# Two early stores cut into 112, 8 and 8 rows, and the last third of q and k in three loads instead of two

## The chip, the cores and the metric

One core of a Trainium2 chip runs the whole program. The metric is device time in microseconds (us), median of several executions. The kernel before takes 254.43 us (three executions: 254.37, 254.43 and 254.54).

The engines are named as in the profile: PE is TensorE (matmuls), PEld its weight loads, DVE is VectorE, ACT is ScalarE, POOL is GpSimd and SP is SyncE. Sixteen DMA engines move the data between memory and SBUF.

## What is computed

Four batches of cross-covariance attention, and a mixture of low-rank adapters on their result:

```python
B, N, C = 4, 6400, 256                      # q, k, v: float32 [B, N, C]
qn = q / (norm(q, axis=1) + 1e-06)          # over the 6400 rows
kn = k / (norm(k, axis=1) + 1e-06)
s = kn.transpose(0, 2, 1) @ qn / tau        # [B, 256, 256]
a = softmax(s, axis=-1)
x = (v @ a).reshape(B * N, C)               # [25600, 256]

logits = x @ w_gate                         # 8 experts
# the two best experts of each row, softmax over the two as weights w
out = x + sum over those two of  w * (x @ A[e]) @ B[e]      # A[e]: 256x16, B[e]: 16x256
```

The norms and the product of a batch need all of its q and k; only then is `a` known, and each row of v can be finished. So for each batch the kernel loads q and k (13.1 MB together in float32), accumulates the Gram products, makes `a`, and then streams v through to the output.

## The kernel before

A list scheduler written in Python at the top of the kernel makes a plan of steps (loads, matmuls, copies, stores), each with an engine and an estimated duration, and simulates them. The order in which its simulation starts the steps is the order in which they are emitted; on each engine the instructions then stand in that fixed order. Changing one load changes the simulation and with it the order of the steps from there on.

The 6400 rows of a batch are laid out as 128 partitions of 50 columns, a column being 256 elements of one row. q and k come in thirds of 17, 17 and 16 columns, v and the output in five pieces of 10 columns:

```python
NC = 50
PC = 10
QK = ((0, 17), (17, 17), (34, 16))
V = ((0, 1), (1, 1), (2, 1), (3, 1), (4, 1))
...
STORE = {"zl": 1, "bank": 6, "qk": 6, "v": 3, "vT": 4, "y": 7, ...}   # buffers of each kind
```

Some thirds are cut further. `PARTS` says how, by batch and third; everything else comes in one load. FINE cuts the last two output pieces:

```python
PARTS = {(0, 0): ((0, 2), (2, 15)), (0, 2): ((34, 8), (42, 8)), (3, 2): ((34, 8), (42, 8))}
FINE = 2
```

In the plan, each part is one load for q and one for k, and the Gram step of a column depends on the part that holds it:

```python
        for c, n in PARTS.get((b, i), QK[i:i + 1]):
            for h in "qk":
                p.add(("load", h, b, i, c, n), {}, (), 0, take=(("qk", (h, b, i)),), size=LOAD * n + 0.062)
...
            for c in range(c0, c0 + n):
                deps = [k for k in p.steps if k[0] == "load" and k[2:4] == (b, i) and k[1] != "v"
                        and k[4] <= c < k[4] + k[5]]
                ...
                p.add(("G", b, c), {"PE": ...}, deps, ...)
```

Loads of q, k and v are issued by GpSimd and cast float32 to bf16 on the way:

```python
    def do_load(s, what, b, i, c, n):
        ...
        nc.gpsimd.dma_start(t[:, c - c0:c - c0 + n, :], src[b, :, c:c + n, :])
```

Some output stores are held back until a given load of k has landed: `HOLD` names the store and the load. A held store stands in SyncE's order behind a tiny DMA that reads the last column of that load, so SyncE waits for it:

```python
HOLD = {(0, 0): ('k', 3, 1), (0, 1): ('k', 1, 2), (0, 4): ('k', 3, 2), (1, 0): ('k', 3, 1),
        (1, 1): ('k', 3, 2), (1, 2): ('k', 3, 2), (1, 3): ('k', 3, 2), (1, 4): ('k', 3, 2),
        (2, 0): ('k', 3, 1), (2, 1): ('k', 3, 2), (2, 4): ('k', 3, 1)}
...
    def do_hold(s, kind, b, i):
        if kind == "k":
            src = held["qk", ("k", b, i), ""][0:1, QK[i][1] - 1, 0:16]
        ...
        nc.sync.dma_start(scrap, src)
```

The store itself is one DMA of 128 partitions (rows, in what follows) from SyncE; a row of a whole piece is 10 columns of 256 float32, 10,240 bytes that lie together in memory:

```python
    out_v = out.rearrange("(b p c) d -> b p c d", b=B, p=P)
...
    def do_store(s, b, i, c, n):
        lo = i * PC + c
        nc.sync.dma_start(out_v[b, :, lo:lo + n, :], held["y", (b, i), ""][:, c:c + n, :])
```

The steps that follow the loads of a batch's q and k, as the profile names them: Gram products (`acc<-qk`), squares on ScalarE (`sq`, `ssq`), their sums on VectorE, the exponentials (`a_exp`), the gate and adapter weights times `a` (`waA`), transposes of v (`T_ps`), the gate's logits (`log`, `ZL`), the gate on VectorE (`gatem` to `gateg`), the low-rank part (`Z`, `gz`, `gzT`), the output product (`Y_ps`) and its copy to SBUF (`y`).

Of the kernel before, what the change touches and what calls it, by code (L numbers as in the profile page):

```python
# [32 lines left out]
class Clock:  # L33


    WINDOW, FIRST, LOW, HIGH = 3.413, 0.31, 0.5, 0.8

# [3 lines left out]
    def at(self, t):  # L41
        w = max(0, int((t - self.FIRST) / self.WINDOW) + 1)
        while len(self.cold) <= w:
            share = self.busy[-1] / self.WINDOW
            self.cold.append(share < (self.HIGH if self.cold[-1] else self.LOW))
            self.busy.append(0.0)
        return w

    def took(self, t, us):

        end, w = t, self.at(t)
        while us > 1e-9:
            pace = 2.0 if self.cold[w] else 1.0
            step = min(us * pace, max(self.FIRST + w * self.WINDOW - end, 1e-6))
            self.busy[w] += step
# [5 lines left out]
    def idle(self, t):  # L61

        w = self.at(t)
        return t - self.FIRST - (w - 1) * self.WINDOW - self.busy[w] > self.SPARE

# [165 lines left out]
def make_plan(B, order, ahead):  # L231
# [6 lines left out]
    for kind, b, i in order:  # L238
        if kind == "v":
            p.add(("load", "v", b, i, V[i][0] * PC, V[i][1] * PC), {}, (), 0, take=(("v", (b, i)),),  # L240
                  size=LOAD * V[i][1] * PC + 0.062)
            continue
# [5 lines that stand above are left out]
        p.add(("cast", h), {"ACT": 0.6}, [("load", h, 0, 0) + PARTS[0, 0][0]], 0)  # L248
    p.loads[2].size += 0.5
    for b in range(B):  # L250

        for i, (c0, n) in enumerate(QK):
# [3 lines that stand above are left out]
                if (b, c) < (0, PARTS[0, 0][0][1]):  # L256
                    deps = [("cast", k[1]) for k in deps]
# [32 lines left out]
        if b == 0:  # L290
            p.add(("wts",), {"DVE": 1.8}, [("load", "k", 0, len(QK) - 1) + PARTS[0, len(QK) - 1][1]], -200)

# [89 lines left out]
    for b in range(B):  # L382
        for i in range(NP):
            x = pos["v", b, max(g for g, (i0, _) in enumerate(V) if i0 <= i)]
            parts = UNITS if b == B - 1 and i >= NP - FINE else ((0, PC),)
            for c, n in parts:
# [23 lines left out]
        (1, 1): ('k', 3, 2), (1, 2): ('k', 3, 2), (1, 3): ('k', 3, 2), (1, 4): ('k', 3, 2),  # L410
        (2, 0): ('k', 3, 1), (2, 1): ('k', 3, 2), (2, 4): ('k', 3, 1)}

PARTS = {(0, 0): ((0, 2), (2, 15)), (0, 2): ((34, 8), (42, 8)), (3, 2): ((34, 8), (42, 8))}
FINE = 2
FIRST = 4
OFF = {(0, 0, 'k'), (0, 0, 'q'), (0, 1, 'q'), (0, 2, 'k'), (0, 2, 'q'), (0, 4, 'q'), (0, 5, 'q'),
        (0, 6, 'k'), (0, 6, 'q'), (0, 7, 'k'), (0, 8, 'q'), (1, 0, 'k'), (1, 0, 'q'), (1, 1, 'q'),
# [41 lines left out]
def kernel(  # L459
# [11 lines left out]
    nc = tc.nc  # L471

    B, N, C = q.shape
    P = 128
# [15 lines left out]
    out_v = out.rearrange("(b p c) d -> b p c d", b=B, p=P)  # L490
# [44 lines left out]
    held = {}  # L535
# [25 lines left out]
    def do_load(s, what, b, i, c, n):  # L561
        if what == "v":
            t, src, c0 = sb(s, "v", (b, i), [P, PC * max(n for _, n in V), C], BF16), v_v, c
        else:
            t = sb(s, "qk", (what, b, i), [P, max(n for _, n in QK), C], BF16)
            src, c0 = {"q": q_v, "k": k_v}[what], QK[i][0]
            if (b, c) == (0, 0):
                n = FIRST
                if "first" not in W:
# [6 lines left out]
        if (what, b, i) in (("q", 0, 0), ("k", 0, 0)):  # L576
            c, n = FIRST, c + n - FIRST
        nc.gpsimd.dma_start(t[:, c - c0:c - c0 + n, :], src[b, :, c:c + n, :])  # L578
# [346 lines left out]

    def do_store(s, b, i, c, n):
        lo = i * PC + c
        nc.sync.dma_start(out_v[b, :, lo:lo + n, :], held["y", (b, i), ""][:, c:c + n, :])


    do = dict(load=do_load, wts=do_wts, sq=do_sq, add=do_add, red=do_red, n2p=do_n2p, hold=do_hold, warm=do_warm, cast=do_cast, G=do_G, accs=do_accs, n2=do_n2, rsqrt=do_rsqrt, rq_ps=do_rq_ps, s=do_s,
              exp=do_exp, recip=do_recip, aT_ps=do_aT_ps, aT=do_aT, waA_ps=do_waA_ps, waA=do_waA,
              a=do_a, ZL=do_ZL, ZLe=do_ZLe, T=do_T, Te=do_Te, log=do_log, loge=do_loge, Z=do_Z, Ze=do_Ze, gzT=do_gzT,
              gzTe=do_gzTe, Y=do_Y, Ye=do_Ye, store=do_store)
    for name in ("m1", "eq1", "lm", "m2", "mask", "msum", "t", "th", "g2"):
        do[name] = gate_step(name)
# [50 lines left out]
```

## Time and profile before

The profile is of one execution with a span of 252.7 us from the first to the last instruction of the program.

| | |
|---|---|
| time, median of 3 | 254.43 us |
| PE busy | 217.8 us (86%) |
| DVE busy | 192.7 us (76%) |
| ACT busy | 151.1 us (60%) |
| POOL busy | 27.1 us (11%) |
| HBM read / written | 78.91 MB / 26.21 MB |
| mean granted TensorE clock | 0.986 |
| the last load of k, columns 42 to 49 of the last batch | landed at 182.94 us |
| the last matmul | ended at 246.8 us |
| the last store | issued at 247.42, landed at 251.95 us |

How to read it. The busy time of an engine is an average over stages, and a high one does not make the engine the bound. The slices of the page cut the span into 40 equal parts; a digit is the busy share in tenths. The DMA row is the mean share of the sixteen DMA engines, and the GB/s row counts the bytes of their packets. Section 3 splits the DMA time by queue: q0 carries what GpSimd issues (the loads), q1 what SyncE issues (nearly all stores), q10 what ScalarE issues, and q8 is the fetching of instructions. A DMA has landed when all its engines have reported; the trace holds the time of each of the sixteen reports, so one can see how far the engines of one DMA lie apart. SyncE does no computing: its waits are listed apart, and they tell what its stores, and at the end the program, waited for.

### The profile page before, as it was taken

The page shows a single profiled execution, that of the slowest core. Times are in us where ns is not written, and L with a number is a line of the kernel's source. Part 1 is how long each engine was busy: PE and PEld are TensorE (multiplying, and loading weights), DVE is VectorE, ACT ScalarE, POOL GpSimd, SP SyncE. Part 2 cuts the span into 40 slices and gives each one's busy share as a digit, 9 for nine tenths or more (in the row PEclk, how much of TensorE's full clock was granted, in tenths as well). Part 3 has the DMA queues.
Part 4 walks back from the last instruction along what each step waited for, and adds up shares of the span by engine and source line. Part 5 has one row for each costly group of instructions (what it writes and reads, how often), then busy time and mean ns, then how long its engine had stood idle before and what let it go on. Part 6 is the DMA issues. An engine that isn't in the chain of part 4 may idle for free.

```text
span 252.7 us, 5852 instructions
## 1 busy us (share of the span) xinstructions
PE 217.8 (86%) x2357; PEld 193.0 (76%) x2357; DVE 192.7 (76%) x528; ACT 151.1 (60%) x269; POOL 27.1 (11%) x54
## 2 busy tenths in 40 slices
PE   0274995988999998689999999889999979999990
PEld 0162882876999996579899899779999769999980
DVE  0055589869899987588899899489898898889850
ACT  5454427546786543975667768362674846657671
POOL 7003010040002002000500100500000000000000
PEclk9998899999999999999999999999999999999997
DMA  8999999999999999999999999999999999999996
GB/s 251 217 217 209 211 223 208 217 218 215 215 217 241 303 305 298 224 213 221 210 215 220 215 217 217 211 212 313 317 251 353 322 341 317 337 392 415 404 408 249
DMA packets 11243, 66.70 MB, mean 264 GB/s; under 512 B 1360, under 2 KB 1744, under 8 KB 6608
## 3 DMA queue, kind: packets, MB, share of 16 engines
q0 software_dynamic: 6912, 38.80, 74.4%
q1 hardware_dynamic: 3968, 26.87, 26.1%
q10 hardware_dynamic: 336, 0.66, 0.8%
q8 instruction: 18, 0.29, 0.4%
q14 instruction: 9, 0.07, 0.1%
HBM read 78.91 MB, written 26.21 MB: 416 GB/s over the span
## 4 chain that ended last, share of the span: by engine, by line
PE 53%; DMA 32%; issue 5%; DVE 4%; ACT 2%; POOL 1%; POOLq 0%; DVEq 0%
DMA v<-in_v_dram 18%; PE Y_ps L915 13%; PE acc L593 10%; DMA qk<-in_q_dram 10%; PE Y_ps L920 6%; PE T_ps L788 5%; PE ZL_ps L812 5%; DMA qk<-in_k_dram 5%; PE gzT_ps L902 4%; PE acc L597 3%; PE acc L602 2%; PE Z_ps L879 1%; ACT a_exp L715 1%; DVE a_bf L763 1%; PE log_ps L826 1%
## 5 line engine op out<-in xcount | busy, mean ns | idle before, releaser
L593 PE MATMUL acc<-qk 128*128 128x256 bf16 x400 | 69.6, 282 | 17.0 <-DMA qk<-in_k_dram 9.4
L915 PE MATMUL Y_ps<-a_bf,vT 128*128 128x256 bf16 x400 | 60.0, 273 | 0.2 <-DVE acc_sb L710 0.2
L621 DVE TENSOR_TENSOR ssq<-ssq,sq 128x1280 f32<-128x1280 f32 (+1 forms) x27 | 43.4, 1606 | 19.6 <-ACT sq L615 19.6
L769 ACT COPY y<-Y_ps 128x512 f32<-128x512 f32 x79 | 46.2, 586 | 16.6 <-PE Y_ps L920 13.5
L593 PEld LDWEIGHTS <-qk 128*128 128x128 bf16 x400 | 34.2, 101 | 20.7 <-DMA qk<-in_k_dram 11.5
L615 ACT ACTIVATE sq<-qk 128x1280 f32<-128x1280 bf16 (+1 forms) x27 | 36.9, 1368 | 17.7 <-DVE ssq L621 16.6
L915 PEld LDWEIGHTS <-vT 128*128 128x128 bf16 x400 | 38.9, 98 | 4.7 <-issue 0.3
L920 PE MATMUL Y_ps<-ball,gzT 128*128 128x256 bf16 x200 | 38.2, 273 | 0.0
L597 PE MATMUL acc<-qk 128*128 128x128 bf16 x242 | 34.5, 224 | 0.0
L788 PE MATMUL T_ps<-ident,v 128*128 128x128 f32 x200 | 27.6, 274 | 0.6 <-DVE waA_sb L757 0.4
L769 ACT COPY vT<-T_ps 128x512 f32<-128x512 f32 (+1 forms) x44 | 21.2, 510 | 10.9 <-PE T_ps L788 10.5
L597 PEld LDWEIGHTS <-qk 128*128 128x128 bf16 x242 | 24.4, 101 | 3.5
L890 DVE TENSOR_TENSOR gz<-zl,gateg 128x256 bf16<-128x256 f32 x70 | 26.3, 445 | 0.3
L578 POOL DMA_DIRECT2D v<-in_v_dram x20 | 11.5, 576 | 133.7 <-PE T_ps L788 92.8
L788 PEld LDWEIGHTS T_ps<-ident,v 128*128 128x128 f32 x200 | 22.3, 141 | 1.6 <-DVE waA_sb L757 0.6
L602 PE MATMUL acc<-qk 128*128 128x128 bf16 x168 | 23.4, 222 | 0.0
L902 PE MATMUL gzT_ps<-ident,gz 128*128 128x128 f32 x100 | 20.9, 281 | 2.6 <-DVE gateg L868 1.4
L920 PEld LDWEIGHTS <-gzT 128*128 128x128 bf16 x200 | 19.6, 98 | 2.3
L812 PE MATMUL ZL_ps<-waA_sb,vT 128*128 128x136 bf16 x280 | 19.5, 223 | 1.7 <-DVE waA_sb L757 1.5
L771 DVE COPY gzT<-gzT_ps 128x256 f32<-128x256 f32 (+1 forms) x40 | 15.0, 380 | 7.1 <-PE gzT_ps L902 5.6
L812 PEld LDWEIGHTS <-vT 128*128 128x128 bf16 x280 | 17.7, 98 | 2.4 <-issue 2.1
L615 ACT ACTIVATE ssq<-qk 128x1536 f32<-128x1536 bf16 x8 | 11.9, 1489 | 11.4 <-DMA qk<-in_q_dram 7.4
(80 smaller groups left out, 271.3 us busy)
## 6 DMA issues: line engine op xcount, KB each, us to landing
out_dram<-y SPq DMA_DIRECT2D x18, 1280.0 KB, 16.7
v<-in_v_dram POOLq DMA_DIRECT2D x20, 640.0 KB, 20.5
qk<-in_q_dram POOLq DMA_DIRECT2D x7, 1088.0 KB, 23.7
qk<-in_k_dram POOLq DMA_DIRECT2D x7, 1088.0 KB, 28.4
qk<-in_q_dram POOLq DMA_DIRECT2D x4, 512.0 KB, 19.2
qk<-in_k_dram POOLq DMA_DIRECT2D x4, 512.0 KB, 22.5
qk<-in_q_dram POOLq DMA_DIRECT2D x2, 1024.0 KB, 19.4
qk<-in_k_dram POOLq DMA_DIRECT2D x2, 1024.0 KB, 23.8
```

What stands on the lines that cost most here:

```text
L593: nc.tensor.matmul(acc[ic][:, 0:256], kt[:, j, ic::CC], qt[:, j, :], start=c == 0, stop=False, skip_group_check=True)
L597: nc.tensor.matmul(acc[ic][:, 256:384], kt[:, j, ic::CC], kt[:, j, ic::CC], start=False, stop=False, skip_group_check=True)
L602: nc.tensor.matmul(acc[ic][:, 384:512], qt[:, j, ic * P:(ic + 1) * P], qt[:, j, ic * P:(ic + 1) * P], start=False, stop=c == NC - 1, skip_ ...
L615: nc.scalar.activation(out[:, 0:n, :], t[:, j:j + n, :], ACT.Square)
L621: nc.vector.tensor_tensor(out=t, in0=t, in1=held["sq", (w, b, g), ""][:, 0:n, :], op=OP.add)
L769: nc.scalar.copy(out, in_)
L788: nc.tensor.matmul(ps[:, j, :], vt[:, c + j, :].bitcast(FP32), W["ident32"], is_transpose=True, start=(j == 0), stop=(j == n - 1))
L812: nc.tensor.matmul(ps[:, j, :], vT_of(b, i, c + j)[:, :, ic], st[b]["waA"][:, ic, :], start=(j == 0 and ic == 0), stop=(j == n - 1 and ic ...
L890: nc.vector.tensor_tensor(out=pairs[:, h].rearrange("p c (e r) -> p c e r", e=E), in0=z[:, 2 * h:2 * h + 2, :].rearrange("p c (e r) -> p c ...
L902: nc.tensor.matmul(ps[:, j, :], pairs[:, j * P:(j + 1) * P], W["ident32"], is_transpose=True, start=(j == 0), stop=(j == n // 2 - 1))
L915: nc.tensor.matmul(ps[:, j, :], vT_of(b, i, c + j)[:, :, ic], st[b]["a"][:, ic, :], start=(j == 0 and ic == 0), stop=False, skip_group_che ...
L920: nc.tensor.matmul(ps[:, j, :], pair[:, :, j], W["B"], start=False, stop=(j == 1), skip_group_check=True)
```

## The change

Two edits. The first cuts the stores of output pieces 0 and 2 of the first batch by rows: 112 rows go by SyncE as before, and two DMAs of 8 rows each are issued by ScalarE. Piece 2 is the first store that the program issues (76.65 us in the profile before), piece 0 is one of two that are released when the second third of the last batch's k has landed (167.45 us). Its purpose is to spread the rows of these stores over the DMA engines in another way. The second edit brings the last third of q and k of the last batch in 8, 5 and 3 columns instead of 8 and 8, so that fewer columns depend on the load that comes last.

```diff
-PARTS = {(0, 0): ((0, 2), (2, 15)), (0, 2): ((34, 8), (42, 8)), (3, 2): ((34, 8), (42, 8))}
+PARTS = {(0, 0): ((0, 2), (2, 15)), (0, 2): ((34, 8), (42, 8)),
+         (3, 2): ((34, 8), (42, 5), (47, 3))}
 FINE = 2
+SPLIT = {(0, 2): (112, 8, 8), (0, 0): (112, 8, 8)}
 FIRST = 4
...
     def do_store(s, b, i, c, n):
         lo = i * PC + c
-        nc.sync.dma_start(out_v[b, :, lo:lo + n, :], held["y", (b, i), ""][:, c:c + n, :])
+        p = 0
+        for rows in SPLIT.get((b, i), (P,)):
+            eng = nc.scalar if p else nc.sync
+            eng.dma_start(out_v[b, p:p + rows, lo:lo + n, :], held["y", (b, i), ""][p:p + rows, c:c + n, :])
+            p += rows
```

The scheduler's simulation sees the second edit and not the first. With it, the order on every engine is the same as before until about the loads in question; on PE the first difference is that the Gram steps of columns 43 and 44 of the last batch stand ahead of a transpose, and from there to the end many steps trade places. The held stores wait for the new last load of k, and the store of piece 0 of the third batch stands ahead of that wait instead of behind it.

## The prediction

> **What bounds the kernel now.** I read the page's slices first, then the queues, then the stretches, then SyncE's own waits, and went to the chain last. The slices:
>
> ```profile
> PE   0274995988999998689999999889999979999990
> ...
> DMA  8999999999999999999999999999999999999996
> GB/s 251 217 217 209 211 223 208 217 218 215 215 217 241 303 305 298 224 213 221 210 215 220 215 217 217 211 212 313 317 251 353 322 341 317 337 392 415 404 408 249
> ```
>
> PE has holes; the DMA row has none between the first slice and the last. GB/s is low only where loads run alone (the packets are counted by the bf16 bytes they write) and rises where stores run. The queues say the same in time:
>
> ```profile
> q0 software_dynamic: 6912, 38.80, 74.4%
> q1 hardware_dynamic: 3968, 26.87, 26.1%
> q10 hardware_dynamic: 336, 0.66, 0.8%
> q8 instruction: 18, 0.29, 0.4%
> ```
>
> 74.4 + 26.1 + 0.8 + 0.4 is over 100% of 16 engines: packets overlap a little and there is no free time. Laying the trace's packets over each other, at no moment from 4 to 238 us are fewer than 16 in flight. The stretches at the end:
>
> ```profile
> 184.00:236.00 52.00, 49.71 (x593) 45.62 (x591) 46.19 (x155) 33.24 (x75) 2.12 (x4) 1.00 1.03 347
> 236.00:241.00 5.00, 5.00 (x52) 4.46 (x51) 4.36 (x16) 3.40 (x8) 0.00 (x0) 1.00 0.93 388
> 241.00:248.00 7.00, 5.77 (x52) 4.95 (x52) 2.20 (x7) 4.94 (x10) 0.00 (x0) 1.00 1.01 413
> 248.00:250.00 2.00, 0.00 (x0) 0.00 (x0) 0.00 (x0) 0.00 (x0) 0.00 (x0) 0.80 0.92 366
> ```
>
> The last two columns are DMA share and GB/s. PE is done at 246.8, yet the DMA share is still 0.92 two us later. What the program waits for at its end stands in SyncE's own waits:
>
> ```profile
> SPq L928 <- ACT y L769: 16.9, 9, 6.0
> ...
> SPq L982 <- DMA out_dram<-y: 3.8, 5, 1.2
> ```
>
> The second line is the end of the kernel waiting for stores that still drain, one after the other. The completion records show it: the last store is issued at 247.42 and its 16 completions (one per DMA engine) come from 249.95 to 251.95. The fastest engine needs 2.5 us and has no backlog; the slowest is 2.0 us behind it. The span of 252.7 us ends 0.7 us after that last completion. **So the end is set by the slowest of 16 DMA engines, busy from its first packet to its last;** PE, which would let the fast engines end at 249.95, comes second by 2 us. The chain in section 4 (PE 53%, DMA 32%) follows compute and does not show this.
>
> How the engines come apart can be read from the loads. A load completes within 0.67 us on all engines at 10.00 us, within 1.66 at 64.94, 2.64 at 166.87. The sixteen completions of each load show single engines dropping back by some 0.9 us each after one of the 18 packets of q8, which take 0.89 to 0.99 us each: one engine fetches 16 KB of instructions while the other fifteen go on. The first eight fetches each hit another engine, the ninth to eleventh make the first ones fall back a second time (three engines at 2.2 to 2.6 us at 161.70). That looks like a cycle over eight engines, while eight have none. At the store that completes at 242.68 the lags behind the fastest are 0, 0.26, 0.36, 0.45, 0.80, 1.10, 1.87, 2.26 for the better half and 2.34 to 3.95 for the worse. Between the means of the halves lie 2.2 us. (The fast ones then run dry for a moment, DMA share 0.93, which is why the last store shows 2.0 us only.)
>
> **What the Trainium skill says.** "DMA: Bandwidth & Descriptors", section "Why a DMA increments its semaphore by 16 and not by 1": a DMA runs on the largest number of engines up to 16 that divides its slowest dimension, and one issued by SyncE or ScalarE takes the lowest-numbered ones. By that 112 rows go to 16 engines, 7 rows each, and 8 rows go to engines 0 to 7, one row each. The trace agrees as far as it can: every store of 128 rows made 16 completions; no DMA on fewer engines is in it. The same page, "Queues, rings and completion order": each engine takes packets in turn from the queues that have work, and SyncE and ScalarE have a queue each. The trace shows both: q1 and q10 stand apart, and loads of 5.2 us become 8 us while stores run (the load of q issued at 77.04 lands 8.3 us after the one before it). "Latency and other measured facts" says that engines 7 and 15 are usually slower; this trace gives engines no numbers, so it can't be checked.
>
> **The change part by part.**
>
> *Split stores.* Before, each engine carries 8 rows of a store of 128. After, engines 8 to 15 carry 7 and engines 0 to 7 carry 7 + 1 + 1 = 9. A row is one packet of 10,240 B; back to back, a store of 8 rows advances each engine by 3.04 us (the last whole stores land at 236.62, 239.64, 242.68), so 0.38 us a row. Two split stores take 2 x 0.38 = 0.76 us from each of engines 8 to 15 and add 0.76 us to each of 0 to 7. That is about a third of the 2.2 us between the halves, if the worse half is 8 to 15.
>
> *What ScalarE pays.* Four DMA issues more; those it has at the start take 0.36 to 0.46 us, so twice about 0.8 us. The first pair stands after the copies of y that end at 76.6, ahead of 1.4 us of waiting for VectorE at 79.46; the second after the exponentials that end at 166.5, ahead of 1.57 us of waiting for the waA product. Both fit in idle time: 0 on the path.
>
> *8 + 8 becomes 8 + 5 + 3.* The bytes stay. Per engine 16 packets of 8 columns become 32 smaller ones. Alone, a load of 17 columns takes 5.155 us a piece (18.43 to 23.59 on the fastest engine) and one of 8 columns 2.46 us (26.09 to 28.55), so 0.300 us a column and 0.06 us for the load itself. Two more loads cost 2 x 0.06 = 0.13 us on every engine. Two more issues by GpSimd (0.5 us each) run 20 us ahead of their data: 0. The first five columns of k come earlier: the eight-column k landed at 182.94, and after the new first part only 8 x 0.134 + 8 x 0.134 us of packets are left, so it should land 1.5 to 2 us sooner, about 181; the last three columns at about 183.
>
> *What moves with it.* The kernel's list scheduler sees the smaller loads. PE's order is the same up to column 42 of the last batch; then columns 43 to 46 go ahead of other work, and the rest of PE's order differs in places to the end. The number of matmuls is unchanged. PE waited for no load after 77 us before (column 42 ran at 183.99, 1.05 us after its load), so there is no DMA wait to remove; PE's idle time from 204 to 247 is 43.00 - 41.08 = 1.9 us in all, 1.4 of it one wait for the gate at 207.5. I give PE's end +-0.8 us. It only counts if PE slips by over 1 us, for the slow engines are that much behind it.
>
> *The sum.* Worse half on 8 to 15: -0.76 + 0.13 = -0.63 us on the engines that end last. The lower half ends no later: 2.26 + 0.76 + 0.13 = 3.15 against 3.95 - 0.63 = 3.32 us. So 254.43 - 0.6 = 253.8.
>
> **The rivals.**
>
> *The slow engines are among 0 to 7, or mixed over both halves.* Nothing in this trace names them. Then the last engine gets 0.76 + 0.13 = 0.9 us more: 255.3. For it: nothing but ignorance. Against it: a split that can only load the lower half is a strange thing to write unless the upper half was seen to lag. I give it 20%.
>
> *PE becomes the bound.* The new order may wait more at the gate and the copies after 195 us. PE's end 1.5 us later would put the last store near 249, its completion on any engine near 251.5, and the time near 254.5. For it: PE is 95 to 100% busy in each of the stretches from 107 to 241 us, so any new hole goes straight to its end. Against it: 1 us of room behind the slow engines. 15%.
>
> *It helps through the loads on the path.* ScalarE waits 3.8 us for the load that lands at 101.49, and PE idles 2.25 us behind it. Were that load 0.4 us earlier, PE would be too. Against it: the stores' queue has work from 78 to 104 us without a break, so a load on an upper engine meets one store packet for each of its own whether the store has 7 rows or 8; and an earlier PE does not free the slow engines. Worth 0 to -0.2 us.
>
> **Range and chances.** Four in five of my weight lies on the first sum, 253.4 to 254.3 by PE's uncertainty; the rest between 254.5 and 255.4. I say 253.85, with 253.2 to 255.3. 2% is 5.1 us; even all 2 us of the backlog would not be that: faster 0.01, same 0.98, slower 0.01.
>
> **What would show it.** Right: the last store's completions lie closer together than 2.0 us, the last one near 251.3 with its issue near 247.4; at the loads around 160 us the spread is about 2.3 instead of 2.64 us (one split behind them); SyncE's waits for out_dram at the end fall under 3.8 us; no DMA wait on PE after 77 us. Wrong: a spread that grows (the halves were the other way round), or a last store issued after 248.5 (PE's order). Wrong altogether would be the prediction if the DMA engines had idle time in the changed kernel before 238 us: then the sum over one engine no longer gives the end.

## The result and the profile after

The changed kernel takes 256.94 us (median of 4 runs, 256.34 to 257.56) against 254.49 us for the kernel before beside it (254.37 to 254.69, 4 runs): ratio 1.0096, 95% interval 1.0071 to 1.0121. It is slower by 2.4 us; predicted were 253.85 and at most 255.3. The profiled execution has a span of 255.0 us.

The same stretches at the end, of the changed kernel (stretch, its length, busy time of PE, PEld, DVE, ACT and POOL, granted clock, DMA share, GB/s):

```profile
184.00:236.00 52.00, 50.38 (x595) 46.25 (x593) 45.93 (x152) 32.83 (x77) 2.84 (x4) 1.00 1.03 340
...
241.00:248.00 7.00, 6.97 (x63) 5.98 (x61) 3.34 (x11) 5.67 (x11) 0.00 (x0) 1.00 1.00 413
248.00:250.00 2.00, 0.00 (x0) 0.00 (x0) 0.00 (x0) 0.59 (x1) 0.00 (x0) 1.00 1.02 413
250.00:255.00 5.00, 0.00 (x0) 0.00 (x0) 0.00 (x0) 0.00 (x0) 0.00 (x0) 0.62 0.34 133
```

PE runs to 247.98 instead of 246.77, and the DMA engines are still full from 248 to 250, where their share was 0.92 before. Both ends have moved. SyncE's own wait at the end of the changed kernel:

```profile
SPq L988 <- DMA out_dram<-y: 4.9, 4, 2.0
```

It was 3.8 us. The last store is issued at 248.62 and its completions come from 251.12 to 254.08: the spread is 2.96 us instead of 2.0.

From the last completion to the end of the span it is 0.97 us, where it was 0.73 before. At its end SyncE waits for eight semaphores (counters that a DMA raises as it lands), one after the other in a fixed order, at 0.06 us for one that is already there. The DMAs of SyncE and ScalarE report to these eight in turn, so with four DMAs more the last store reports to another one: four checks come after its own, and before there was none. SyncE's DRAIN behind the checks, before and after (count, ns, first and last start); the last completions are at 251.95 and 254.08:

```profile
L982 SPq DRAIN  x2: 7/7/7, 252.0 to 252.1; - x2
```

```profile
L988 SPq DRAIN  x2: 7/7/7, 254.4 to 254.5; - x2
```

So 0.24 us of the loss has nothing to do with when the stores land. It is the same in every profile below with both stores in 112, 8 and 8 rows; where two DMAs are added (112 + 16 rows, or one store split) six checks follow and the end is 0.37 us longer; with whole stores it stays at 0.72 to 0.74.

The queues of the changed kernel (packets, MB, share of 16 engines' span):

```profile
q0 software_dynamic: 7200, 38.80, 74.3%
q1 hardware_dynamic: 3936, 26.54, 25.7%
q10 hardware_dynamic: 400, 0.99, 1.3%
```

The last line is ScalarE's queue. It gained 32 rows of 10,240 B, and its share rose by 0.5% of 16 x 255 us = 20 us, so about 0.64 us for each row, against the 0.38 of the prediction. The packet records agree: the 32 rows took 0.65 us in the mean, the median 0.4, the longest 2.12. This is time in flight, and packets overlap in it (the three shares add up to 101.3%).

Where the lateness begins can be followed through the waits. First the kernel before, then the changed one, ScalarE's wait and TensorE's (sum, times, longest):

```profile
ACT ssq L615 <- DMA qk<-in_q_dram: 7.4, 2, 3.8
...
PE aT_ps L729 <- ACT a_exp L715: 2.2, 1, 2.2
```

```profile
ACT ssq L617 <- DMA qk<-in_q_dram: 8.8, 2, 4.7
...
PE aT_ps L731 <- ACT a_exp L717: 3.5, 2, 3.1
```

The load of q for batch 2 lands on its fastest engine at 98.21 us (98.22 before), on its slowest at 102.39 (101.49 before). ScalarE squares it ahead of batch 1's exponentials, so they start 0.9 us later, and TensorE, which transposes their result, resumes at 104.78 instead of 103.88. After it TensorE's clock is halved for 3.4 us. One line each of the stretch 104 to 108, before and after:

```profile
104.00:108.00 4.00, 3.56 (x39) 3.11 (x38) 3.41 (x8) 3.21 (x6) 0.00 (x0) 1.00 1.01 209
```

```profile
104.00:108.00 4.00, 3.22 (x18) 2.52 (x19) 1.57 (x5) 3.67 (x7) 0.00 (x0) 0.57 0.99 203
```

18 matmul records stand there in place of 39, in part because TensorE resumes only 0.8 us into the stretch. From there it is 1.8 us late. And then that lateness reaches the DMA engines. GpSimd's timeline, the first of the loads of batch 3's last third, before and after (start, length, what it waited for):

```profile
160.76 0.53 POOL L578 DMA_DIRECT2D qk<-in_q_dram  x1 [17.32 <-ACT acc_sb L651]
```

```profile
162.59 0.53 POOL L580 DMA_DIRECT2D qk<-in_q_dram  x1 [17.32 <-ACT acc_sb L653]
```

GpSimd had been waiting 17 us for a buffer of q and k. The view names ScalarE's copy of batch 2's sums, but it is TensorE's last Gram product of batch 2 that frees the buffer: in all 19 profiles the issue comes 0.53 or 0.54 us after that product ends, and in one (the split with the exponentials first, below) it comes ahead of that copy:

```profile
159.47 0.53 POOL L582 DMA_DIRECT2D qk<-in_q_dram  x1 [17.30 <-PE acc L606]
```

So all 1.83 us pass from TensorE to the loads. The fastest DMA engine is through with the load ahead of them at 164.23 and 164.03: the first issue was 3.5 us ahead of that before and is 1.4 us ahead now. What that does, before and after:

```profile
163.00:166.00 3.00, 3.00 (x35) 2.68 (x34) 2.03 (x5) 1.56 (x4) 1.47 (x3) 1.00 1.00 207
170.00:172.00 2.00, 2.00 (x28) 1.86 (x26) 2.00 (x4) 0.39 (x1) 0.00 (x0) 1.00 1.07 260
```

```profile
163.00:166.00 3.00, 2.99 (x32) 2.66 (x32) 1.84 (x13) 1.34 (x1) 3.00 (x7) 1.00 0.96 187
170.00:172.00 2.00, 1.24 (x21) 1.24 (x21) 1.39 (x5) 1.66 (x2) 0.72 (x1) 1.00 1.09 158
```

The DMA share dips (0.96, 187 GB/s), which is no more than 0.12 us of empty engines in the 3 us. From 170 to 172 the engines are "busy" but move 158 GB/s, less than the 205 to 225 of loads alone elsewhere in the page's slices: packets are in flight for longer. The store that lands at 236.62 us in the kernel before is complete at 234.48 in the mean of its 16 engines; in the changed kernel the store of the same place in the order is at 236.29. The DMA engines have lost 1.8 us, well before the end, and that comes on top of the 0.24 us behind the last completion.

### The profile page after: what moved, and what is told of

The parts are those of the page before. It is cut to its first block, busy times and chain, and to the rows that moved or that the text cites. A ratio compares the mean times of both kernels' runs of the same rounds, so it can differ in the third digit from the quotient of the medians.

```text
span 255.0 us, 5863 instructions
## 1 busy us (share of the span) xinstructions
PE 218.9 (86%) x2357; PEld 193.6 (76%) x2357; DVE 192.2 (75%) x526; ACT 151.0 (59%) x271; POOL 29.2 (11%) x56
## 4 chain that ended last, share of the span: by engine, by line
PE 53%; DMA 32%; issue 5%; DVE 3%; ACT 2%; POOL 1%; POOLq 0%
DMA v<-in_v_dram 17%; PE Y_ps L917 13%; PE acc L595 10%; DMA qk<-in_q_dram 10%; PE Y_ps L922 7%; PE ZL_ps L814 5%; DMA qk<-in_k_dram 5%; PE T_ps L790 5%; PE gzT_ps L904 4%; PE acc L599 3%; PE acc L604 2%; PE Z_ps L881 2%; DVE a_bf L765 2%; ACT a_exp L717 1%; PE log_ps L828 1%
## 5 line engine op out<-in xcount | busy, mean ns | idle before, releaser
L917 PE MATMUL Y_ps<-a_bf,vT 128*128 128x256 bf16 x400 | 60.8, 275 | 0.0
L771 ACT COPY vT<-T_ps 128x512 f32<-128x512 f32 (+1 forms) x46 | 22.1, 517 | 9.3 <-PE T_ps L790 9.1
L580 POOL DMA_DIRECT2D v<-in_v_dram x20 | 12.6, 629 | 126.8 <-PE T_ps L790 119.0
L790 PE MATMUL T_ps<-ident,v 128*128 128x128 f32 x200 | 26.4, 274 | 0.0
L904 PE MATMUL gzT_ps<-ident,gz 128*128 128x128 f32 x100 | 22.0, 286 | 1.2 <-DVE gz L892 1.0
```

The costliest lines, as they stand in the source:

```text
L771: nc.scalar.copy(out, in_)
L790: nc.tensor.matmul(ps[:, j, :], vt[:, c + j, :].bitcast(FP32), W["ident32"], is_transpose=True, start=(j == 0), stop=(j == n - 1))
L904: nc.tensor.matmul(ps[:, j, :], pairs[:, j * P:(j + 1) * P], W["ident32"], is_transpose=True, start=(j == 0), stop=(j == n // 2 - 1))
L917: nc.tensor.matmul(ps[:, j, :], vT_of(b, i, c + j)[:, :, ic], st[b]["a"][:, ic, :], start=(j == 0 and ic == 0), stop=False, skip_group_che ...
```

## The experiments

All times are medians, the ratio is to the kernel before run beside each (254.34 to 254.40 us), with its 95% interval. The right half is from one profiled execution of each: the wait of TensorE near 104 us, the first issue of the last third's loads, the end of TensorE, the first and last completion of the last store. "Exponentials first" is a change of order on ScalarE, which the two kernels with whole stores by ScalarE have too; "later" is further work on ScalarE. Both are described below.

| kernel | us | ratio | wait | issue | PE ends | completions |
|---|---|---|---|---|---|---|
| smaller loads alone | 254.52 | 0.9998 to 1.0014 | none | 160.45 | 245.84 | 249.00 to 251.90 |
| split alone | 256.61 | 1.0078 to 1.0119 | 3.36 | 162.60 | 248.60 | 251.77 to 252.98 |
| split, all by SyncE | 254.78 | 1.0013 to 1.0031 | none | 159.27 | 245.90 | 249.05 to 251.84 |
| 112 + 16 rows | 255.34 | 1.0021 to 1.0045 | 3.08 | 162.37 | 248.38 | 251.52 to 252.45 |
| first store split | 255.95 | 1.0037 to 1.0082 | 3.87 | 163.19 | 249.21 | 252.35 to 253.66 |
| second store split | 255.17 | 1.0017 to 1.0038 | 1.91 | 160.61 | 246.63 | 249.76 to 252.28 |
| split, exponentials first | 255.45 | 1.0039 to 1.0077 | none | 159.47 | 248.15 | 251.33 to 252.40 |
| before, exponentials first | 254.35 | 0.9992 to 1.0008 | none | 158.80 | 245.89 | 249.06 to 251.80 |
| before, 1 us later | 254.85 | 1.0012 to 1.0035 | 1.93 | 161.59 | 247.61 | 250.76 to 251.74 |
| change, exponentials first | 256.13 | 1.0059 to 1.0091 | none | 161.28 | 250.07 | 253.22 to 254.65 |
| change, all by SyncE | 255.32 | 1.0022 to 1.0044 | 2.14 | 161.45 | 246.83 | 250.00 to 252.06 |
| exponentials first, whole third | 254.38 | 0.9991 to 1.0007 | none | 158.55 | 246.68 | 250.50 to 251.75 |
| 112 + 16 rows, exponentials first | 254.76 | 1.0014 to 1.0034 | none | 158.78 | 246.07 | 249.22 to 251.85 |
| whole stores by ScalarE | 254.23 | 0.9988 to 1.0004 | none | 158.88 | 246.34 | 249.50 to 251.65 |
| before, 2.1 us later | 256.83 | 1.0058 to 1.0103 | 1.58 | 161.18 | 247.19 | 250.35 to 251.80 |
| before, 3.6 us later | 257.50 | 1.0092 to 1.0154 | 2.08 | 163.01 | 249.02 | 252.17 to 254.17 |
| whole by ScalarE, whole third | 254.96 | 1.0013 to 1.0034 | none | 160.36 | 248.34 | 252.15 to 252.87 |

### The two parts of the change, each alone

The loads of 8, 5 and 3 columns with the stores whole: the new `PARTS` and the old `do_store`.

> The kernel before with the loads in 8, 5 and 3 columns and whole stores. Theory A (the split rows load DMA engines that were the slow ones already): this part costs two more loads of 0.06 us, so about 254.6 us; the load of q that ScalarE waits for lands at 101.5 us and PE's idle time behind it stays 2.25 us. Theory B (the smaller loads and the new order of the steps are what costs): 256 to 257 us, and the completions of the loads and stores from 172 us on lie as far apart as in the changed kernel (7.9 us at the five-column k).

254.52 us: at most a few tenths (0.9998 to 1.0014). The load of q landed at 98.48 us here and TensorE did not wait. The split with the loads as they were:

```diff
+SPLIT = {(0, 2): (112, 8, 8), (0, 0): (112, 8, 8)}
 # and the new do_store; PARTS as before
```

> The kernel before with the two stores as 112 rows by SyncE and twice 8 by ScalarE, loads in 8 and 8. Theory A: 0.76 us more on the engines that end last, 255.3 us, and up to 256.5 us if PE's later start at 103 us is not made good; the load of q lands near 102.3 us, PE waits 3.1 us behind it and its clock drops to half for one window; the last store's completions spread over 2.8 us. Theory B: 254.5 us.

256.61 us, nearly all of the loss, and with the same late issue at 162.60 us as the change. So the stores are the cause and the smaller loads are not.

### What of the split costs: rows or the queue

The same split with every piece by SyncE (`eng = nc.sync`), so the same 9 and 7 rows on the engines:

> As the run with the split alone, but all three pieces are issued by SyncE, so that the rows per DMA engine are the same (9 and 7) and no third queue takes turns with the loads. If rows per engine are what counts (theory A): the engines that end last still get 0.76 us more, 255.3 us, and the spread at the load of k that landed at 106.96 us grows from 1.84 to about 2.6 us; but the load of q lands at 101.5 us again and PE's wait behind it is 2.25 us. If ScalarE's queue is what counts: 254.5 us and a spread of 1.84 us.

254.78 us: 0.4 and not 2.3, and 0.24 of it is SyncE's longer end; the last completion, at 251.84, is no later than before. TensorE has no wait at 104, and none of SyncE's 10,240 B rows takes over 1.0 us. Then 16 rows in one piece by ScalarE, `SPLIT = {(0, 2): (112, 16), (0, 0): (112, 16)}`, so that every engine has 8 rows again:

> As the run with the split alone, but in 112 rows by SyncE and one piece of 16 rows by ScalarE, so that each of the 16 engines carries 8 rows again. Theory A (rows per engine): 254.5 us, spread at the load of k near 1.84 us; the third queue takes one packet on every engine, so the load of q lands 0.4 us later, at 101.9 us, and PE waits 2.6 us. If issuing from ScalarE or its queue is what costs: 255.5 to 256.5 us.

255.34 us, with the wait of 3.08 us and the halved clock, although no engine carries a row more than before. Nine of ScalarE's 32 rows took over 0.6 us, up to 1.62. So unequal rows are not needed for a loss. But the pieces of 8 rows lose 1.3 us more (256.61), and they differ in the rows on an engine and in the number of pieces. Each store split alone:

> The kernel before with only the store of piece 2 of the first batch (at 76.6 us) split, 112 by SyncE and twice 8 by ScalarE. Theory C (the third queue delays the load of q that ScalarE waits for, PE then starts 0.9 us later, falls to half clock for 3.4 us, and ends some 1.7 us later): the load lands at 102.3 us, PE's wait is 3.1 us, its last matmul ends near 248.5 us, and the time is about 255.2 us, as in the run with 112 and 16 rows. Theory D (what costs is the second split, where packets are stretched while three queues share an engine): 254.5 us.

> The kernel before with only the store of piece 0 of the first batch (released at 167 us) split, 112 by SyncE and twice 8 by ScalarE. Theory C: PE's wait near 104 us is 2.25 us again, no half clock there, PE ends at 246.8 us, and the time is 254.5 us. Theory D: packets between 167 and 190 us take 10 us or more beyond their usual time in sum, the stores after 200 us land 0.5 to 1.5 us later than before, and the time is 255.0 to 256.0 us.

The first (255.95 us) has the whole chain, wait, halved clock and issue at 163.19; the second (255.17 us) has no longer wait, no halved clock and no late issue, and its load packets took 1.2 us in sum beyond their median, as before, where 10 us or more were expected. It still costs 0.8, in its profiled execution too: 0.37 at SyncE's end, 0.33 by a last completion at 252.28 in place of 251.95. The load of q, on its slowest engine, landed at 101.23 to 103.00 us in the seven profiles with the first store's pieces on ScalarE, and at 98.48 to 101.68 in the twelve others.

### Taking the late start away

The square of the delayed q is moved behind batch 1's exponentials on ScalarE, a change of order alone:

```diff
+    at = [s.key for s in steps]
+    late = steps.pop(at.index(("sq", "q", 2, 0)))
+    steps.insert(at.index(("exp", 1, 1)), late)
```

In the split alone, and as a control in the kernel before:

> The run with the split alone (256.61 us), with one step moved on ScalarE: the square of the delayed q stands behind the exponentials of the batch before, so that they no longer wait for that load. Theory C: PE's wait near 104 us goes, and with it most of the loss: 254.8 us, as with the split by SyncE. Theory D: PE ends at 246.8 us or earlier, yet the time stays at 255.5 to 256.6 us.

> The kernel before with the same step moved on ScalarE and nothing else. PE's wait of 2.25 us near 104 us goes and PE ends 1 to 2 us earlier, at 245 to 246 us. If the DMA engines set the end: the last store still lands near 251.9 us and the time is 254.3 us, within 0.2. If PE sets the end: 252.5 to 253.5 us.

The split falls from 256.61 to 255.45 us, so 1.2 us of its loss went through the wait at 104. In its profiled execution another load had one engine far behind (158.31 us), ScalarE squared that load ahead of a copy, and TensorE idled 1.80 us behind it up to 160.74, with its clock halved from 162.2 to 165.6: the same pattern at another place. The kernel before gains nothing (254.35), though its TensorE ends 0.9 us sooner: there the slowest DMA engine does set the end, as the prediction had it. Then in the whole change:

> The whole change, with the square of the delayed load of q moved behind batch 1's exponentials on ScalarE. Theory of the late TensorE: no idle time over 1 us at 104, no halved clock, last loads of q and k issued near 161, and only the uneven rows and the two more loads are left: 254.8 to 255.3. Theory that ScalarE's queue costs the same wherever TensorE stands: 256.3 to 257.

256.13 us, where up to 255.3 was expected: 0.8 of the loss goes, more than expected stays. The profiled execution of this one (257.42 us, the longest of the six, the others 255.80 to 256.40) shows why something stays. TensorE's wait, of this kernel:

```profile
PE T_ps L793 <- DMA v<-in_v_dram: 2.1, 1, 2.1
```

This was no wait before. At the load of v issued at 60.18 us one engine is 5.34 us behind the fastest and the next 3.47; at the load before it the whole spread was 1.36. Between the two, two of ScalarE's rows took 2.32 and 1.76 us. Up to 168 us the slowest engine stays 4.7 to 5.9 us behind the fastest. And the whole change with SyncE issuing all pieces:

> The whole change, with the pieces of 8 rows issued by SyncE behind the 112 rows, so that they stand in the stores' queue and no third queue asks for turns. Theory of the third queue: the load of q lands near 99 to 100 us, no idle time of TensorE at 104, and the time is that of the split on SyncE (254.78) plus the two more loads (0.15 to 0.2): 254.9 to 255.0. Theory that the rows of 9 and 7 to an engine cost it: as the change, 256.5 to 257.

255.32 us, against 254.78 without the smaller loads: 0.3 over the expected. Against that theory the load of q landed at 101.42 and TensorE waited 2.14 us, with its clock halved; the issue at 161.45 was not late. Here three of SyncE's rows took 1.30 to 1.73 us near 176.

### The queue or the small pieces

Both with the exponentials first: 16 rows in one piece by ScalarE, and the two stores whole, 128 rows each, by ScalarE:

```diff
-        nc.sync.dma_start(out_v[b, :, lo:lo + n, :], ...)
+        eng = nc.scalar if (b, i) in ((0, 2), (0, 0)) else nc.sync
+        eng.dma_start(out_v[b, :, lo:lo + n, :], ...)
```

> Stores split as 112 rows by SyncE and 16 by ScalarE, 8 rows to every engine as before, and the square of q behind the exponentials. Theory that ScalarE's rows cost because only 8 engines carry them: 254.35 to 254.5, as with the moved square alone. Theory that single rows from ScalarE's queue are slow on the engine that takes them, whatever their number per engine: 254.8 to 255.4, with rows of up to 1.5 us among ScalarE's in the trace.

> The same two stores whole, 128 rows each, by ScalarE, and the square of q behind the exponentials. No row or issue is added, the two stores only stand in another queue. Theory that the number of queues asking at once is what costs: 255 or more. Theory that the small pieces cost it, one or two rows to an engine that all start together: 254.3 to 254.6, all rows at 0.40 us.

254.76 us, five of eight runs at 254.57 to 254.79 and three at 255.35 to 255.43; and 254.23 us, as the kernel before or a shade under. ScalarE's queue in the second:

```profile
q10 hardware_dynamic: 624, 3.29, 3.2%
```

256 rows more than before for 2.4% more: 97 us / 256 = 0.38 a row, where the changed kernel's came to 0.64. A third queue with rows to carry costs nothing here.

Of the 0.4 us of the 16 rows, 0.37 are SyncE's longer end. The last completion is at 251.85, with the stores whole and in SyncE's queue at 251.80; what follows it, of the 112 + 16 rows:

```profile
L990 SPq DRAIN  x2: 7/7/7, 252.3 to 252.4; - x2
```

Its 32 rows on ScalarE took 0.43 us in the mean and 1.01 at most. So in this execution (254.74 us, one of the five) the even pieces cost the DMA engines nothing, as the first theory said; what the three longer runs lost is not known. The pieces of 8 rows, in the same queue and order, take 255.45, which is 0.7 us more. Whether that comes from half of the engines carrying them or from twice the number of pieces, no run tells.

### A late start alone, with the DMA work of before

Squares of a few columns more are put on ScalarE ahead of the exponentials. They write values again that are there already, so nothing else differs:

```diff
         nc.scalar.activation(out[:, 0:n, :], t[:, j:j + n, :], ACT.Square)
+        if (w, b, g) == ("q", 2, 0):
+            nc.scalar.activation(out[:, 0:4, :], t[:, j:j + 4, :], ACT.Square)
```

with 4 columns (1 us), 6 + 2 columns (2.1 us) and 6 + 6 + 2 columns (3.6 us):

> The kernel before with nothing of the change, and one further Square of four columns on ScalarE (about 1 us, its values are written a second time by the Square that follows) ahead of batch 1's exponentials. Theory that a late TensorE is what the change costs: TensorE's idle time at 104 us grows from 2.25 to about 3.2 us, its clock is halved for about 3.4 us after it, the loads of the last thirds are issued about 1.8 us later, TensorE ends near 248.5 us, and the time is 255.0 to 255.6. Theory that the two extra queue pieces themselves cost it, through the DMA engines: the late TensorE is swallowed by the 2 us of backlog of the slowest engine, and the time stays at 254.4 to 254.6.

> The kernel before with about 2.1 us of further Square on ScalarE ahead of batch 1's exponentials, its values written again by nothing else and unchanged; the DMA work is that of before. Theory of the late start: TensorE idles 3 to 4 us at 104 us, its clock is halved for 3.4 us, it ends near 249, the last store is issued near 249.7, and the time is 255.5 to 256. Theory that the slowest engine's backlog still covers it: 254.4 to 254.9.

> The kernel before with about 3.6 us of further Square on ScalarE ahead of batch 1's exponentials, the DMA work that of before. If the late start is the cause: TensorE idles about 3 to 4.5 us at 104 us even with an early load of q, its clock is halved after it, GpSimd issues the loads of the last third at 162.5 or later, the DMA share between 163 and 166 falls under 0.97, TensorE ends at 249 or later, and the time is 257 to 258 in all executions. If the earlier spread had another cause: again times from 254.3 upward with a wait that was long.

254.85, 256.83 and 257.50 us. The first lies between its two theories, the second is worse than the 255.5 to 256 expected, and the third, expected at 257 to 258 in all executions, goes from 255.94 to 259.32. In the kernel before the load of q lands now early, now late (98.5 to 101.5 us in the profiles of kernels whose DMAs are the same up to there), and so the runs spread: with 2.1 us they go from 254.32 to 257.71, and the profiled one was the fastest, with an issue at 161.18 and no loss; the profiled one of the first (254.25) was the fastest too. With 3.6 us the chain is there in the profile. GpSimd's issue and the stretches, of this kernel:

```profile
163.01 0.53 POOL L578 DMA_DIRECT2D qk<-in_q_dram  x1 [17.33 <-ACT acc_sb L655]
```

```profile
163.00:166.00 3.00, 2.57 (x29) 2.40 (x29) 2.25 (x15) 1.76 (x2) 2.99 (x6) 1.00 0.91 165
170.00:172.00 2.00, 1.11 (x21) 0.99 (x19) 1.39 (x4) 1.67 (x2) 0.00 (x0) 1.00 1.06 142
```

The same two marks as in the changed kernel, deeper, with not a byte, row or queue different from the kernel before. GpSimd's load packets that started between 120 and 190 us took 26.0 us in sum beyond the median of their size, counting those over by 0.1 us and more (1.2 in the kernel before, 15.9 in the changed one). (26.0 - 1.2) / 16 engines = 1.55 us; as an estimate, 3 x (1.00 - 0.91) = 0.27 us of empty engines come to that. The store that is complete at 234.48 us in the mean in the kernel before is so at 236.13, 1.65 us later, which is of that size. For the changed kernel the same estimate gives (15.9 - 1.2) / 16 = 0.9 us; with 0.12 us of empty engines, 32 x (0.65 - 0.38) / 16 = 0.5 us for ScalarE's rows and 0.13 us for two loads more it comes to 1.7 of its 1.8 us. **A late TensorE costs DMA time.** With the 3.6 us it was expected that the clock be halved, and it was not: the wait was 2.08 us. The halved clock only makes TensorE later and is not needed for the loss.

By the issue of the last third's loads the profiles fall in two groups. Issued at 161.6 us or earlier, the load packets lost 0.9 to 3.3 us in sum; at 162.37, 162.59, 162.60, 163.01 and 163.19 it was 8.8, 15.9, 13.8, 26.0 and 18.8. The fastest engine was through with the load ahead at 164.22 in the kernel with the issue at 161.59, and at 164.23 in that with 162.37. Some 2.6 us ahead was enough, 1.9 us was not. No run delays these issues and nothing else, so that it is the issue, and not something that comes with a late TensorE, is an inference from the two groups.

### Versions that might beat both

Two loads fewer, q and k of the last batch's last third whole, with the exponentials first; and the same with the two whole stores by ScalarE:

> The kernel before with the square of q moved behind batch 1's exponentials, and with the last third of q and k of the last batch in one load of 16 columns each instead of 8 and 8, so two loads fewer. If a load costs every engine 0.06 us and the engines set the end, 254.35 - 0.13 = 254.2. If TensorE then waits for the 16 columns of k, which land about 1.2 us later than the first eight did, and loses more than it has in hand, 255 or more.

> The two early stores whole on ScalarE, the square of q behind the exponentials, and q and k of the last third of the last batch in one load each. Whole stores on ScalarE took 254.23, and two loads fewer save 0.13 us by the estimate, though they showed no gain before: 254.1 to 254.3, no difference to the kernel before that matters.

254.38 us, no gain, and 254.96, where 254.1 to 254.3 was expected: TensorE ends at 248.34 there, late enough to set the end, after one wait of 1.8 us for the gate on VectorE that the other does not have. None of the runs beats the kernel before beyond its interval.

## Why the prediction was wrong

**The bound of the kernel before** was read rightly: a TensorE that ends 0.9 us sooner gains nothing (254.35).

**The step that failed** is about TensorE: "It only counts if PE slips by over 1 us, for the slow engines are that much behind it." That takes the DMA engines' end as fixed while TensorE moves. It isn't: GpSimd's loads wait for TensorE's Gram products, and with TensorE 1.8 us late at 162 us they were issued 1.8 us later, their packets took 15.9 us in sum beyond the usual, and the stores after them were complete 1.8 us later. The backlog that was to cover the slip moved with it. The overlap was misread in "run 20 us ahead of their data: 0". From the issue at 162.33 to the landing at 182.94 it is 20 us, but the fastest engine was through with the load ahead of the group at 164.23, only 3.5 us after the group's first issue, and a slip of 1.8 us used up half of that.

Of the marks named in the prediction two came plainly: the spread grew from 2.00 to 2.96 us, and the last store was issued at 248.62, after 248.5. The third, idle DMA engines before 238 us, came only as the share of 0.96 from 163 to 166 us. In the rival "PE becomes the bound" a sum was off as well: a last completion at 251.5 is a time of 254.0 by the kernel before (254.43 - 251.95 = 2.48), not 254.5.

**The rival that was argued away** led there. That "a load on an upper engine meets one store packet for each of its own" is an argument for engines 8 to 15. The load is complete when its last engine is, and an engine with ScalarE's rows now meets those too: the load's fastest engine is as before, its slowest 0.9 us later. The sign of "0 to -0.2 us" was wrong. Between moving the exponentials ahead or not lie 1.2 us in the split alone and 0.8 us in the change.

**The rows.** "-0.76" from engines 8 to 15 presumed that they lag. No run shows such a gain. The spread of the load that lands near 167 us, which was to shrink from 2.64 to 2.3, is 2.61 to 4.82 in the seven profiles with the first store in 112, 8 and 8 rows, and 2.20 to 2.64 in the ten with it whole. The split by SyncE is 0.4 us slower than before, and 0.24 of that is SyncE's longer end, a term that the prediction held fixed ("ends 0.7 us after that last completion"). That 8 rows do run on eight engines, as the Trainium skill says ("DMA: Bandwidth & Descriptors", "Why a DMA increments its semaphore by 16 and not by 1"), the trace now shows: each such DMA has eight completions in place of sixteen. Whether they are the lowest-numbered it doesn't show.

**The cost of a row** on ScalarE was put at 0.38 us and was 0.65 of time in flight in the mean. The same page, "Issuing engines are not separate DMA queues", says that issuing from several engines saves only sequencer time. With whole stores that holds (254.23); with pieces of 8 rows the same bytes cost 0.7 to 0.8 us more from ScalarE than from SyncE, the wait near 104 already taken out (255.45 against 254.78, 256.13 against 255.32), which the section does not speak of. In both profiles TensorE was late behind another load. Why single rows are held up to 2.3 us, and why less often in SyncE's queue, stays open.

**ScalarE's issues** were put at 0 on the path; no run shows otherwise, though the second pair came at 172.15 us, ahead of another wait than the prediction named. **The smaller loads** were put at 0.13 us: 254.52 - 254.34 = 0.2 us alone, within its interval of -0.05 to 0.4, but 0.5 together with the split by SyncE. The first five columns of k were to land at about 181 us. With the smaller loads alone they did, at 180.85; in the changed kernel, where the loads were issued late, at 184.23.

The loss in steps, each from the median of one kernel to the next (254.4, 254.78, 255.32, 256.13, 256.94): 0.4 for the pieces by SyncE, with the 0.24 of the longer end in it, 0.5 for the smaller loads with them, 0.8 for the pieces in ScalarE's queue, 0.8 for the wait near 104; together 2.5 us. The steps are rough: the whole change by SyncE (255.32) has a wait near 104 itself, and the one with the exponentials first (256.13) is late behind another load.

## What to carry to other kernels

Backlog on the DMA engines is no reserve for a late compute engine when that engine frees the buffers of the next loads: ask how long before the engines need a load it is issued, and what the issue waits for (here 2.6 us ahead was enough and 1.9 us was not). A load is as late as its slowest engine, so a few small pieces beside it can move a wait on the path though the engines carry no more bytes. Before a few tenths of a us are put down to the transfers, look at what follows the last completion: a DMA more or less can move the last store to another place in the final checks (0.24 and 0.37 us here). Before stores are cut to even out engines, show which engines lag.

## What the runs showed of the hardware

- Rows of a DMA that has one of them to an engine were in flight for up to 2.3 us from ScalarE's queue, not in every run (at most 0.88 to 1.01 us in three profiles), where the rows of the two whole stores took 0.39 us in the mean and 0.78 at most from the same queue. In one execution an engine was left 2 to 3 us further behind and nothing made it up for 80 us.
- Load packets that were issued late were slower while they were in flight, not only later: in the changed kernel 38 of the 256 packets of 2,560 B, of 0.21 us otherwise, took 0.1 to 0.6 us more near 171 us. The cause was not found; it was so in all five profiles with the late issue.
- A DMA of 8 rows from SyncE or ScalarE shows nine updates of its semaphore, one some 0.4 to 0.7 us after the issue and eight as its rows land; one of 16, 112 or 128 rows shows sixteen, all as they land.
- TensorE's clock was halved for some 3.4 us after waits of 1.93, 2.14, 3.08, 3.15, 3.36 and 3.87 us near 104 us, and not after 1.58, 1.91, 2.08 and 2.25 us; it was after 1.80 us at 160.74 in one run. "TensorE: Matmul & The Clock Gate", section "HAM oscillation — how this bites in real kernels", of the Trainium skill warns of gaps over some 3.4 us; here shorter ones did it, and for this kernel the measurement counts; the length of the gap alone doesn't tell.
